# Seven block products in place of eight for the last three chunks of a gated feed-forward kernel, with the sums on VectorE

## Chip, cores, metric

One core of one Trainium2 chip. The metric is device time in microseconds (us). A profiled run also gives a span, from the first to the last recorded instruction, some 2 us shorter than the time. No die can be compared with another here.

In the lines of a profile PE is TensorE, PEld its weight loads, DVE VectorE, ACT ScalarE, POOL GpSimd and SP SyncE; `L504` is a line of the kernel. The change moves the lines: gate/value matmuls are L487 before and L505 after, gates L504 and L521, the attention multiplies that come in pairs ("the L472 pair" below) L452 and L472, the last step of `xT` L411 and L431, output products of 512 columns L514 and L530. New are the block products (L592), token sums (L586) and weight sums (L561).

## What is computed

An attention stage gives `x`, 4608 tokens of 512 features. The part that matters is the feed-forward product behind it:

```python
def _moe_ref(x, w_gate, w_val, w_out):      # 4608 x 512, 512 x 1536 (twice), 1536 x 512
    gate = np.maximum(x @ w_gate, 0.0)
    val = x @ w_val
    return (gate * val @ w_out).astype(np.float32)
```

## The kernel before

The kernel works in 36 slots. A token chunk has 512 tokens and takes four slots; each slot makes three of the chunk's twelve gate/value tiles (`emit_h`, 128 of the 1536 hidden features each) and one 128-token tile of the output product of the previous chunk (`emit_y`). Slots 0 to 27 carry attention work as well, slots 28 to 35 do not; I call these the tail. After slot 35 the last chunk's output product stands alone. A tile's gate is the step in which ScalarE and VectorE read the tile's two products out of PSUM, where the matmuls put their results in banks of 512 columns, and multiply them into SBUF. `xT` is the transposed `x` that the tiles read, in four quarters of 128 features; its last quarter is finished only 2.6 us into slot 28.

```python
def emit_h(c, jj, pp, parts=((0, range(4)), (1, range(4)))):
    h1, h2 = pair(pp)[:, 0, :], pair(pp)[:, 1, :]    # a pair is two PSUM banks
    for which, kks in parts:
        emit_h_mm(c, jj, pp, which, kks)             # 128x512 matmuls: w_gate into h1, w_val into h2
    def gate():
        r1 = ffn.tile([128, TCH], FP16, name="r1", tag="r1")
        nc.scalar.activation(out=r1, in_=h1, func=AF.Relu)
        gt = gpool.tile([128, TCH], FP16, name="gT", tag="gT")
        nc.vector.tensor_tensor(out=gt, in0=r1, in1=h2, op=ALU.mult)
        gts[c, jj] = gt
    return gate

def emit_y(c, ty, bank, cut=0, inner=None):
    # ... 12 matmuls of 512 columns into one bank, then
    nc.scalar.copy(out=y_sb, in_=y_ps)
    emit_out(c, ty, y_sb, nc.scalar)

# emit_slot, slots without attention:
    if gate: gate()                                  # third gate of the slot before
    emit_y(c - 1, s % 4, 2)
    emit_h(c, jj, 0)()                               # pair 0
    emit_h(c, jj + 1, 1)()                           # pair 1
    return emit_h(c, jj + 2, 0)                      # pair 0; its gate comes in the next slot

# after slot 35:
    gate()
    for ty in range(3):
        emit_y(NCH - 1, ty, ty)
    emit_y_last(NCH - 1, 3, 3)                       # two halves of 256 columns
```

The softmax here doesn't subtract the row's maximum and nothing guards it: scores larger than these inputs give would overflow.

## Time and profile before

| | before |
|---|---|
| time, median of 3 runs | 357.89 us (357.83 to 358.13) |
| span of the profiled run | 356.0 us |
| slot 28 starts | 279.70 us |
| last matmul starts | 352.14 us |
| TensorE busy | 97% |

### The profile page before, as it was taken

The page shows a single profiled execution, that of the slowest core. Times are in us where ns is not written, and L with a number is a line of the kernel's source. Part 1 is how long each engine was busy: PE and PEld are TensorE (multiplying, and loading weights), DVE is VectorE, ACT ScalarE, POOL GpSimd, SP SyncE. Part 2 cuts the span into 40 slices and gives each one's busy share as a digit, 9 for nine tenths or more (in the row PEclk, how much of TensorE's full clock was granted, in tenths as well). Part 3 has the DMA queues.
Part 4 walks back from the last instruction along what each step waited for, and adds up shares of the span by engine and source line. Part 5 has one row for each costly group of instructions (what it writes and reads, how often), then busy time and mean ns, then how long its engine had stood idle before and what let it go on. Part 6 is the DMA issues. An engine that isn't in the chain of part 4 may idle for free.

```text
span 356.0 us, 7222 instructions
## 1 busy us (share of the span) xinstructions
PE 346.9 (97%) x2851; PEld 177.8 (50%) x2851; DVE 226.4 (64%) x344; ACT 211.9 (60%) x358; POOL 188.7 (53%) x233
## 2 busy tenths in 40 slices
PE   6999999999999999999999999999999999999995
PEld 2665555545555455555555555555554444444443
DVE  5894666687786677777777888877775523222220
ACT  3867775676666777766666666666666532322321
POOL 8986557999999877777778877711000000000000
PEclk9999999999999999999999999999999999999999
DMA  9999999999999999999999999930000100000022
GB/s 150 168 171 187 181 196 157 176 175 180 163 166 170 154 130 130 132 130 131 129 135 133 131 133 119 119 92 31 31 30 23 38 30 29 31 29 29 31 59 89
DMA packets 167170, 40.25 MB, mean 113 GB/s; under 512 B 149888, under 2 KB 162656, under 8 KB 167136
## 3 DMA queue, kind: packets, MB, share of 16 engines
q0 software_dynamic: 132960, 22.93, 85.6%
q1 hardware_dynamic: 28832, 7.53, 15.0%
q10 hardware_dynamic: 5344, 9.34, 7.7%
q8 instruction: 22, 0.36, 0.4%
q14 instruction: 12, 0.10, 0.1%
HBM read 46.45 MB, written 9.44 MB: 157 GB/s over the span
## 4 chain that ended last, share of the span: by engine, by line
PE 90%; DVE 4%; ACT 3%; DMA 1%; issue 1%; DVEq 0%; POOLq 0%
PE ps L487 51%; PE ps L514 25%; PE ps L428 3%; PE ps L228 2%; PE ps L294 2%; PE ps L283 2%; PE ps L436 2%; DMA qk<-in_k_dram 1%; DVE xn L406 1%; ACT rden L403 1%; DVE xo L355 1%; ACT rden L405 1%; PE ps L544 1%; DVE ee L306 1%; ACT r L502 1%
## 5 line engine op out<-in xcount | busy, mean ns | idle before, releaser
L504 DVE TENSOR_TENSOR gT<-r,ps 128x512 f16<-128x512 f16 x108 | 71.9, 684 | 67.3 <-PE ps L487 45.5
L487 PE MATMUL ps<-xT,wg_sb 128*128 128x512 f16 x432 | 111.3, 379 | 0.9 <-DVE xn L406 0.8
L487 PE MATMUL ps<-xT,wv_sb 128*128 128x512 f16 x432 | 111.0, 379 | 0.0
L514 PE MATMUL ps<-wo_sb,gT 128*128 128x512 f16 x420 | 100.1, 380 | 0.0
L502 ACT ACTIVATE r<-ps 128x512 f16<-128x512 f32 x108 | 64.0, 593 | 33.5 <-PE ps L487 30.8
L452 DVE TENSOR_TENSOR xn<-ps,rden 64x720 f16<-64x720 f32 x46 | 41.6, 905 | 42.5 <-ACT rden L449 41.8
L487 PEld LDWEIGHTS <-wv_sb 128*128 128x128 f16 x432 | 42.2, 98 | 50.7
L487 PEld LDWEIGHTS <-wg_sb 128*128 128x128 f16 x432 | 39.8, 97 | 44.4 <-issue 0.7
L514 PEld LDWEIGHTS <-gT 128*128 128x128 f16 x420 | 39.1, 98 | 45.5
L303 ACT ACTIVATE ee<-ps 112x576 f16<-112x576 f32 x64 | 38.1, 647 | 26.2 <-PE ps L294 25.4
L522 ACT COPY y_sb<-ps 128x512 f32<-128x512 f32 x35 | 20.5, 587 | 46.9 <-PE ps L514 46.9
L446 ACT ACTIVATE rden<-ps 64x720 f32<-64x720 f32 x46 | 35.2, 764 | 12.8 <-PE ps L436 12.2
L306 DVE TENSOR_TENSOR ee<-ee,cst_sb 112x576 f16<-112x576 f16 x64 | 40.9, 677 | 1.3 <-ACT ee L303 1.1
L255 POOL TENSOR_TENSOR vd<-v 72x256 f16<-72x256 f32 x23 | 17.1, 745 | 44.1 <-PE ps L436 43.5
L174 POOL DMA_DIRECT2D qk<-in_q_dram x46 | 34.2, 745 | 4.3 <-DMA wo_sb<-in_moe_w_out_dram 2.8
L174 POOL DMA_DIRECT2D qk<-in_k_dram x46 | 33.3, 729 | 0.5 <-DMA vw<-in_v_dram 0.3
L195 POOL DMA_DIRECT2D vw<-in_v_dram x30 | 28.4, 948 | 4.7 <-PE ps L228 1.5
L209 DVE TENSOR_REDUCE qkd<-qkT 128x288 f16<-128x1152 f16 x23 | 30.9, 1342 | 0.0
L254 POOL TENSOR_TENSOR v<-v 72x512 f32<-72x512 f16 x23 | 30.2, 1314 | 0.3
L411 DVE TENSOR_TENSOR xT<-xn 128x576 f16<-128x576 f16 x28 | 22.4, 799 | 0.2
L428 PE MATMUL ps<-ee,vw 112*128 112x96 f16 x276 | 20.3, 205 | 0.4 <-DVE ee L306 0.4
L312 ACT ACTIVATE ed<-ps 72x576 f16<-72x576 f32 x32 | 20.5, 642 | 0.0
(77 smaller groups left out, 288.7 us busy)
## 6 DMA issues: line engine op xcount, KB each, us to landing
out_dram<-y_sb ACTq DMA_DIRECT2D x34, 256.0 KB, 3.7
vw<-in_v_dram POOLq DMA_DIRECT2D x30, 168.0 KB, 6.2
qk<-in_q_dram POOLq DMA_DIRECT2D x46, 72.0 KB, 3.6
qk<-in_k_dram POOLq DMA_DIRECT2D x46, 72.0 KB, 3.7
v<-in_v_dram POOLq DMA_DIRECT2D x23, 144.0 KB, 6.1
wg_sb<-in_moe_w_gate_dram POOLq DMA_DIRECT2D x4, 384.0 KB, 9.7
wv_sb<-in_moe_w_val_dram POOLq DMA_DIRECT2D x4, 384.0 KB, 10.5
wo_sb<-in_moe_w_out_dram POOLq DMA_DIRECT2D x4, 384.0 KB, 12.1
```

The source lines that it names most:

```text
L174: nc.gpsimd.dma_start(dv[:, :, hh, :], _dap(src, off + hh * S * D, [[D, 96], [NQ * D, NB], [1, D]]),)
L209: nc.vector.tensor_reduce(out=qkd[hp % 2].rearrange("p i t -> p (i t)"), in_=qkT[hp % 4][:, 0 : 2 * S].rearrange("p (t f) -> p t f", f=4), ...
L254: nc.gpsimd.tensor_tensor(out=m, in0=t[:, :, 0:128], in1=t[:, :, 128:256], op=ALU.add)
L303: nc.scalar.activation(out=o, in_=ps[0:WK, p0 + 2 * g : p0 + 2 * g + 2, 0:288], func=AF.Exp, scale=scale)
L306: nc.vector.tensor_tensor(out=o, in0=o, in1=_sap(masks_sb, (0, WK), 288 * g, [[0, 2], [1, 288]]), op=ALU.mult,)
L428: nc.tensor.matmul(out=ps[:, bank, NQ * j : NQ * j + NQ], lhsT=vflat[:, v0 : v0 + 128], rhs=e[:, hh, lo : lo + NQ], start=True, stop=True,)
L446: nc.scalar.activation(out=r[lo : lo + 64], in_=ps[de : de + 64, 4 + 2 * hh : 6 + 2 * hh, 0:360], func=AF.Ln)
L452: nc.vector.tensor_tensor(out=x[lo : lo + 64], in0=ps[lo : lo + 64, 4 + 2 * hh : 6 + 2 * hh, 0:360], in1=r[lo : lo + 64], op=ALU.mult,)
L487: nc.tensor.matmul(out=pair(pp)[:, which, :], lhsT=w[:, kk, bass.ts(jj, 128)], rhs=xT[:, kk, c * TCH : (c + 1) * TCH], start=(kk == 0), st ...
L502: nc.scalar.activation(out=r1, in_=h1, func=AF.Relu)
L504: nc.vector.tensor_tensor(out=gt, in0=r1, in1=h2, op=ALU.mult)
L514: nc.tensor.matmul(out=y_ps, lhsT=gts[c, jj][:, bass.ts(ty, 128)], rhs=wo_sb[:, jj, :], start=(jj == 0), stop=(jj == NJJ - 1),)
```

## The change

Intent: the output product of chunks 6, 7 and 8 as a Strassen scheme (Winograd's form). 256 tokens and 512 outputs are two by two blocks, the 1536 hidden features two halves; seven block products take the place of eight, so 42 matmuls of 256 columns do what 24 of 512 did. It needs four sums of gate blocks per 256 tokens and four sums of w_out blocks once, all fp16 on VectorE. One weight sum goes into each of slots 24 to 27, the token sums into every second slot of the tail (the last chunk's into slot 35 and behind it). Products accumulate on each other in PSUM, and ScalarE copies intermediate values out between.

```diff
-    gpool = ctx.enter_context(tc.tile_pool(name="gpool", bufs=24))
+    gT = ring(2, [128, NJJ, TCH], FP16, "gT_")           # gates of a chunk as one tile
+    wt, sa, sums = ...                                   # scratch in retired attention buffers (cut)
+    def emit_wt(i):                                      # four weight sums, 128 x 1536 each
+        o, a, b = ((t1, b12, b11), (t2, b22, t1), (t3, b22, b12), (t4, b21, t2))[i]
+        nc.vector.tensor_tensor(out=o, in0=a, in1=b, op=ALU.subtract)
+    class Unit:                                          # 256 tokens; banks a, b, d
+        def sums(self, lo=0, hi=NK, which=range(4)):     # NK = 6
+            ops = ((s1, a21, a22, ADD), (s2, s1, a11, SUB), (s3, a11, a21, SUB), (s4, a12, s2, SUB))
+            for o, a, b, op in (ops[i] for i in which):
+                nc.vector.tensor_tensor(out=o[:, lo:hi, :], in0=a[:, lo:hi, :], in1=b[:, lo:hi, :], op=op)
+        # mm(out, left, right, first): 6 matmuls of 256 columns; first clears, otherwise it accumulates
+        # p1: a = A11 B11, copied to m1          p2: d = A12 B21; y11 = d + m1
+        # p6: a += S2 T2, copied to m2           p5: b = S1 T1
+        # p7: a += S3 T3, copied to m3; y22 = b + m3
+        # p4: a += A22 T4; y21 = a               p3: b += S4 B22; y12 = b + m2
+    def emit_tail_slot(s, gate):
+        c, jj = s // 4, 3 * (s % 4)
+        gate()
+        if s % 2 == 0:
+            w = units[c - 1] = Unit(c - 1, s % 4 // 2, (4, 5, 6))
+            w.sums()
+            w.p1()
+            if s == NP - LEAD:                           # slot 28
+                emit_h_mm(c, jj, 0, 0, range(3))
+                emit_h_mm(c, jj, 0, 1, range(3))
+                w.p2()
+                emit_h(c, jj, 0, ((0, range(3, 4)), (1, range(3, 4))))()
+            else:
+                emit_h(c, jj, 0)(); w.p2()
+            emit_h(c, jj + 1, 1)()
+            w.p6(); w.p5()
+        else:
+            # ... p7, tile jj, p4, tile jj + 1, p3; in slot 35 also last[0].sums(0, 4), last[1].sums(0, 4)
+        return emit_h(c, jj + 2, 0)
     # after slot 35
-    for ty in range(3):
-        emit_y(NCH - 1, ty, ty)
-    emit_y_last(NCH - 1, 3, 3)
+    # p1 of both units, the sums' slices 4 and 5, then p2, p6, p5, p7, p4, p3, each for both units
```

More of the change, by code (lines that the diff above doesn't have):

```diff
@@ L85 @@
     NVP = 9
+    NK = NJJ // 2
     B0 = 1
@@ L94 @@
     ffn = ctx.enter_context(tc.tile_pool(name="ffn", bufs=3))
-    gpool = ctx.enter_context(tc.tile_pool(name="gpool", bufs=24))
+    ypool = ctx.enter_context(tc.tile_pool(name="ypool", bufs=4))
     zero_sb = keep.tile([128, 640], FP16, name="zero_sb")
@@ L112 @@
     NV4 = 5
-    qk16 = ring(NL, [96, 2, 2 * NB * 64], FP16, "qk16_")
+    qkfull = ring(NL, [128, 2, 2 * NB * 64], FP16, "qk16_")
+    qk16 = [t[0:96] for t in qkfull]
     v4 = ring(NV4, [72, 4, 256], FP16, "v4_")
-    v2 = ring(2, [72, 4, 128], FP32, "v2_")
-    vw = ring(NL, [WK, 2 * NB, 128], FP16, "vw_")
+    v2full = ring(2, [128, 4, 128], FP32, "v2_")
+    v2 = [t[0:72] for t in v2full]
+    vwfull = ring(NL, [128, 2 * NB, 128], FP16, "vw_")
+    vw = [t[0:WK] for t in vwfull]
     qkT = ring(4, [128, 2 * S + 32], FP16, "qkT_")
@@ L125 @@
     ones_sb = keep.tile([128, 128], FP16, name="ones_sb")
-    q32 = keep.tile([96, 2 * NB * 64], FP32, name="q32")
+    q32full = keep.tile([128, 2 * NB * 64], FP32, name="q32")
+    q32 = q32full[0:96]
+    gT = ring(2, [128, NJJ, TCH], FP16, "gT_")
     xT = keep.tile([128, NPB, NTOK], FP16, name="xT")
     ps = psum.tile([128, 8, 512], FP32, name="ps")
+    wt = [
+        t.rearrange("p i c -> p (i c)").rearrange("p (j d) -> p j d", d=256) for t in qkfull[0:4]
+    ]
+    sa = [
+        [vwfull[r].rearrange("p b c -> p (b c)")[:, 768 * i : 768 * (i + 1)]
+         .rearrange("p (j t) -> p j t", t=128) for r in rs for i in range(2)]
+        for rs in ((4, 5), (6, 0))
+    ]
+    v2flat = [t.rearrange("p a b -> p (a b)") for t in v2full]
+    sums = [
+        [q32full[:, 256 * i : 256 * (i + 1)] for i in range(3)],
+        [v2flat[0][:, 0:256], v2flat[0][:, 256:512], v2flat[1][:, 0:256]],
+    ]
     nc.scalar.preload_act_table_set("natural_log_exp_and_others")
@@ L480, in emit_x_pe @@
             nc.vector.tensor_copy(out=o, in_=pair(pp)[:, :, 0:288])
-    gts = {}
     def emit_h_mm(c, jj, pp, which, kks):
@@ L502, in gate @@
             nc.scalar.activation(out=r1, in_=h1, func=AF.Relu)
-            gt = gpool.tile([128, TCH], FP16, name="gT", tag="gT")
-            nc.vector.tensor_tensor(out=gt, in0=r1, in1=h2, op=ALU.mult)
-            gts[c, jj] = gt
+            nc.vector.tensor_tensor(out=gT[c % 2][:, jj, :], in0=r1, in1=h2, op=ALU.mult)
         return gate
@@ L515, in emit_y @@
                 out=y_ps,
-                lhsT=gts[c, jj][:, bass.ts(ty, 128)],
+                lhsT=gT[c % 2][:, jj, bass.ts(ty, 128)],
                 rhs=wo_sb[:, jj, :],
@@ L520, in emit_y @@
             )
-        y_sb = ffn.tile([128, D_MODEL], FP32, name="y_sb", tag="y_sb")
+        y_sb = ypool.tile([128, D_MODEL], FP32, name="y_sb", tag="y_sb")
         nc.scalar.copy(out=y_sb, in_=y_ps)
@@ L535, in emit_out @@
             done += n
-    def emit_y_last(c, ty, bank):
-        y_sb = ffn.tile([128, D_MODEL], FP32, name="y_sb", tag="y_sb")
-        for i, (copy, eng) in enumerate(
-            ((nc.scalar.copy, nc.scalar), (nc.vector.tensor_copy, nc.sync))
-        ):
-            lo, hi = 256 * i, 256 * i + 256
-            for jj in range(NJJ):
-                nc.tensor.matmul(
-                    out=ps[:, bank + i, 0:256],
-                    lhsT=gts[c, jj][:, bass.ts(ty, 128)],
-                    rhs=wo_sb[:, jj, lo:hi],
-                    start=(jj == 0),
-                    stop=(jj == NJJ - 1),
-                )
-            copy(out=y_sb[:, lo:hi], in_=ps[:, bank + i, 0:256])
-            emit_out(c, ty, y_sb, eng, lo, hi)
+    halves = [
+        [wo_sb[:, NK * i : NK * (i + 1), 256 * k : 256 * (k + 1)] for k in range(2)] for i in range(2)
+    ]
@@ new lines, in emit_wt, with __init__, mm, p1 @@
+    def emit_wt(i):
+        (b11, b12), (b21, b22) = halves
+        t1, t2, t3, t4 = wt
+        o, a, b = ((t1, b12, b11), (t2, b22, t1), (t3, b22, b12), (t4, b21, t2))[i]
+        nc.vector.tensor_tensor(out=o, in0=a, in1=b, op=ALU.subtract)
+    class Unit:
+        def __init__(self, c, u, banks):
+            self.c, self.u = c, u
+            self.a, self.b, self.d = (ps[:, k, 0:256] for k in banks)
+            self.s1, self.s2, self.s3, self.s4 = sa[u]
+            self.m1, self.m2, self.m3 = sums[u]
+            g = gT[c % 2]
+            self.x = [
+                [g[:, NK * i : NK * (i + 1), 256 * u + 128 * t : 256 * u + 128 * t + 128] for i in range(2)]
+                for t in range(2)
+            ]
+        def sums(self, lo=0, hi=NK, which=range(4)):
+            (a11, a12), (a21, a22) = self.x
+            ops = (
+                (self.s1, a21, a22, ALU.add),
+                (self.s2, self.s1, a11, ALU.subtract),
+                (self.s3, a11, a21, ALU.subtract),
+                (self.s4, a12, self.s2, ALU.subtract),
+            )
+            for o, a, b, op in (ops[i] for i in which):
+                nc.vector.tensor_tensor(
+                    out=o[:, lo:hi, :], in0=a[:, lo:hi, :], in1=b[:, lo:hi, :], op=op
+                )
+        def mm(self, out, left, right, first):
+            for i in range(NK):
+                nc.tensor.matmul(
+                    out=out,
+                    lhsT=left[:, i, :],
+                    rhs=right[:, i, :],
+                    start=(first and i == 0),
+                    stop=(i == NK - 1),
+                    skip_group_check=True,
+                )
+        def p1(self):
+            self.y = [
+                ypool.tile([128, D_MODEL], FP32, name="y_sb", tag="y_sb") for _ in range(2)
+            ]
+            self.mm(self.a, self.x[0][0], halves[0][0], True)
+            nc.scalar.copy(out=self.m1, in_=self.a)
+        def p2(self):
+            self.mm(self.d, self.x[0][1], halves[1][0], True)
+            nc.vector.tensor_tensor(out=self.y[0][:, 0:256], in0=self.d, in1=self.m1, op=ALU.add)
+            self.out(0, 0)
+        def p6(self):
+            self.mm(self.a, self.s2, wt[1], False)
+            nc.scalar.copy(out=self.m2, in_=self.a)
+        def p5(self):
+            self.mm(self.b, self.s1, wt[0], True)
+        def p7(self):
+            self.mm(self.a, self.s3, wt[2], False)
+            nc.scalar.copy(out=self.m3, in_=self.a)
+            nc.vector.tensor_tensor(out=self.y[1][:, 256:512], in0=self.b, in1=self.m3, op=ALU.add)
+            self.out(1, 1)
+        def p4(self):
+            self.mm(self.a, self.x[1][1], wt[3], False)
+            nc.scalar.copy(out=self.y[1][:, 0:256], in_=self.a)
+            self.out(1, 0)
+        def p3(self):
+            self.mm(self.b, self.s4, halves[1][1], False)
+            nc.vector.tensor_tensor(out=self.y[0][:, 256:512], in0=self.b, in1=self.m2, op=ALU.add)
+            self.out(0, 1)
+        def out(self, t, k):
+            emit_out(self.c, 2 * self.u + t, self.y[t], nc.sync, 256 * k, 256 * k + 256)
@@ L599, in emit_fill @@
         emit_warm(1)
+    units = {}
+    def emit_tail_slot(s, gate):
[11 more added lines that the diff above has]
+            else:
+                emit_h(c, jj, 0)()
+                w.p2()
+            emit_h(c, jj + 1, 1)()
+            w.p6()
+            w.p5()
+        else:
+            w = units[c - 1]
+            w.p7()
+            emit_h(c, jj, 0)()
+            w.p4()
+            if s == 4 * NCH - 1:
+                last[0].sums(0, 4)
+            emit_h(c, jj + 1, 1)()
+            w.p3()
+            if s == 4 * NCH - 1:
+                last[1].sums(0, 4)
+        return emit_h(c, jj + 2, 0)
     def emit_slot(s, gate):
@@ L636, in emit_slot @@
             emit_h(c, jj, 0)()
+            if 24 <= s < 28:
+                emit_wt(s - 24)
             if hp < NP:
@@ L673 @@
         gate = None
-        for s in range(NCH * 4):
+        for s in range(NP - LEAD):
             gate = emit_slot(s, gate)
+        gate = lambda: None
+        last = [Unit(NCH - 1, u, b) for u, b in ((0, (4, 5, 6)), (1, (7, 2, 3)))]
+        for s in range(NP - LEAD, NCH * 4):
+            gate = emit_tail_slot(s, gate)
         gate()
-        for ty in range(3):
-            emit_y(NCH - 1, ty, ty)
-        emit_y_last(NCH - 1, 3, 3)
+        for x in last:
+            x.p1()
+        for which in (range(2), range(2, 4)):
+            for x in last:
+                x.sums(4, NK, which)
+        for p in ("p2", "p6", "p5", "p7", "p4", "p3"):
+            for x in last:
+                getattr(x, p)()
 _INS = ['q', 'k', 'v', 'moe_w_gate', 'moe_w_val', 'moe_w_out']
```

## The prediction

> **What bounds the kernel now.** I began with the page, parts 1, 2 and 4: busy time, the slices, and the chain of work that ended last.
>
> ```profile
> PE 346.9 (97%) x2851; PEld 177.8 (50%) x2851; DVE 226.4 (64%) x344; ACT 211.9 (60%) x358; POOL 188.7 (53%) x233
> ...
> DVE  5894666687786677777777888877775523222220
> ...
> PEclk9999999999999999999999999999999999999999
> ...
> PE 90%; DVE 4%; ACT 3%; DMA 1%; issue 1%; DVEq 0%; POOLq 0%
> PE ps L487 51%; PE ps L514 25%; PE ps L428 3%; PE ps L228 2%; PE ps L294 2%; PE ps L283 2%; PE ps L436 2%; DMA qk<-in_k_dram 1%; DVE xn L406 1%; ACT rden L403 1%; DVE xo L355 1%; ACT rden L405 1%; PE ps L544 1%; DVE ee L306 1%; ACT r L502 1%
> ```
>
> The reader is to see that TensorE is busy 97% of the span at full clock and that 90% of the last chain is TensorE work. A matmul taken away shortens the kernel, so long as nothing else fills its place. VectorE falls to two or three tenths in the last eight to nine slices, which are the stage that the change fills. That stage begins at 279.70 us (slot 28 of 36, the first without attention) and reads like this in the timeline of the last 26 us:
>
> ```profile
> 339.27 1.03 PE L487 MATMUL ps<-xT,wv_sb 128*128 128x512 f16 x4
> ...
> 341.86 7.93 PE L514 MATMUL ps<-wo_sb,gT 128*128 128x512 f16 x36
> 342.13 0.69 DVE L504 TENSOR_TENSOR gT<-r,ps 128x512 f16<-128x512 f16 x1 [1.04 <-PE ps L487]
> ...
> 349.42 2.72 PEld L544 LDWEIGHTS <-gT 128*128 128x128 f16 x24
> 349.63 2.78 PE L544 MATMUL ps<-wo_sb,gT 128*128 128x256 f16 x24
> ...
> 352.50 0.42 DVE L551 COPY y_sb<-ps 128x256 f32<-128x256 f32 x1 [9.69 <-DMA out_dram<-y_sb]
> 352.96 0.34 SPq L531 DMA_DIRECT2D out_dram<-y_sb  x1
> ```
>
> From this come the two prices that matter. The length shown for a group includes the latency of its last matmul (means 379 ns at 512 columns, 272 ns at 256, in the groups by line). So one 512-column matmul takes (7.93 - 0.38)/35 = 0.2157 us from start to start, and one of 256 columns (2.78 - 0.27)/23 = 0.1091 us: half, with no penalty. Weight loads are 98 ns each, under 109, so they still hide, narrowly. The output of the last product ends at 352.25; copy, DMA and the closing barrier bring the span to 356.0, a tail of 3.75 us.
>
> For VectorE the page's mean misleads, and I asked for the groups by form between 240 and 280 us:
>
> ```profile
> L504 DVE TENSOR_TENSOR gT<-r,ps 128x512 f16<-128x512 f16 x12 | 7.9, 685 | 3.9 <-PE ps L487 3.0 <-ACT r L502 0.7
> L306 DVE TENSOR_TENSOR ee<-ee,cst_sb 112x576 f16<-112x576 f16 x8 | 3.3, 452 | 0.0
> L411 DVE TENSOR_TENSOR xT<-xn 128x576 f16<-128x576 f16 x4 | 3.0, 752 | 0.0
> ```
>
> An fp16 sum of 576 elements out of SBUF takes 452 ns here (677 on the page, whose mean includes the GpSimd-heavy part), where the same length with a broadcast operand takes 752.
>
> **What the Trainium skill says.** "TensorE: Matmul & The Clock Gate", section "Wait — 56ns, not 53.3ns?": warm start-to-start is N/2.4 GHz plus about 2.5 ns. That gives 215.8 and 109.2 ns; the trace agrees. "VectorE: DVE Perf Modes", section "What auto-detection actually checks": a tensor_tensor whose tensors are all 16-bit with unit step runs at two elements per cycle. The trace agrees: 452 against 752 ns. Every weight sum and token sum of the change has this form (fp16, unit innermost step). "SBUF — State Buffer", section "Who interferes with whom": VectorE operations with two SBUF inputs and GpSimd operations that read SBUF exclude each other. The inflated 677 ns mean fits this; GpSimd shows no work after 258 us, so the token sums should not be held.
>
> **The change, part by part.**
>
> *Removed and put in, TensorE.* One unit is 256 tokens by 512 outputs. Before: 2 x 12 matmuls of 512 columns, 24 x 0.2157 = 5.18 us. After: 7 products x 6 matmuls of 256 columns, 42 x 0.1091 = 4.58 us. Six units (chunks 6, 7, 8): 6 x 0.60 = 3.6 us. The scheme saves 1/8 of these matmuls' time and adds no weight-load time. The combinations of products accumulate in PSUM by starting without a clear, at no matmul cost.
>
> *Added, VectorE, hidden.* From the 452 ns I take (N/2 + 145)/0.96. Four weight sums of 1536 elements cost 0.95 us each, one in each of slots 24 to 27. The instruction order puts each between a gate multiply and the L452 pair, where VectorE idles about 2 us waiting for ScalarE's reciprocal (10.2 us over ten instructions, all before the first of each pair). So 0.95 us fits, and even 1.75 us at one element per cycle would.
>
> Four token sums per unit, 768 elements: 0.55 us each, about 2.1 us together, in every second slot of the tail. That slot lasts 3 x 1.73 + 4 x 0.65 = 7.8 us and VectorE has 3 gates (2.1 us), one 256-column output sum (0.42) and the sums (2.1): 4.6 of 7.8. The gate that frees the next PSUM pair is ordered ahead of the sums. The next gate is late by about 0.6 us, but its second bank is wanted only 3 us later. The first product P1 reads raw gates and P6 is two gate/value pairs later, so neither waits for the sums.
>
> *Slot 28.* Here xT's last quarter comes late, at 282.30 us before. The new order covers it with P1, six matmuls of the first three quarters and P2: 0.65 + 1.29 + 0.65 = 2.6 us from 279.70, just to 282.3. I allow 0 to 0.1 us of wait.
>
> *Last slot and end.* VectorE must do gate 9, four sums of 512 elements (about 1.5 us), gate 10, an output sum, four more sums and gate 11. Taking slot 35's start as zero: gate 9 is ready at 2.65 and done at 3.34, sums to 4.85, gate 10 from 5.03 to 5.72, output sum to 6.15, sums to 7.65, gate 11 to 8.3. TensorE ends its value matmuls at 7.13, runs P1 of both units to 8.44, and asks for gate 11 only in the sixth matmul of P2, at 9.0. A margin of 0.7 us. The remaining slices of the sums are eight of 256 elements (0.28 us each), of which P6 wants only the first four, at 9.75 or later. Afterwards the two units alternate, so a PSUM bank has 0.65 us to be read by ScalarE (0.20 to start, 0.37 for the copy) before it is accumulated on again: 0.57 plus a semaphore, about even. Allow 0.1 us for both units.
>
> The last chunk's matmuls are 84 x 0.1091 = 9.16 us, against 36 x 0.2157 + 24 x 0.1091 = 10.38: this 1.2 is already in the 3.6. Then comes an output sum of 256 columns from PSUM (0.42 us, as the 512-column multiply's 685 ns scales), where a copy of 0.42 us was, and the same 128 KB DMA from SP. So the tail stays 3.75 us, give or take 0.2. Output DMAs come every 0.65 us at the end, with SP issues of 0.34 us; they keep up.
>
> Sum: -3.6 TensorE, +0.1 slot 28, +0.1 the interleaved end, about 0 tail: -3.4 to -3.5 us. 357.9 - 3.5 = **354.4 us**, 1% less. Scratch tiles reuse attention buffers after their last use, so nothing earlier should move.
>
> **Rivals.** *(a) VectorE becomes the bound in the tail.* If fp16 sums ran at one element per cycle, 768 elements would be 0.95 us and the even slot's VectorE 6.3 us, still under 7.8. But in slot 35, gate 11 would end near 9.4 instead of 8.3 and TensorE would stall about 0.5 us: 355.0. L306's 452 ns speaks against it; the strided halves of w_out and gates have the same unit inner step, but no instruction of before has just these patterns.
>
> *(b) The narrow matmuls do not hold 109 ns.* If weight loads (98 ns) stopped hiding behind 109 ns, for instance with semaphore waits standing on loads, each narrow matmul would cost 10 to 20 ns more. Then 252 x 10 to 20 ns = 2.5 to 5 us, and the gain would be gone: 356.9 to 359.4. The 24 matmuls of L544 speak against it, as they ran two groups back to back without a gap.
>
> *(c) The end is longer.* Eight small outputs, each waiting for an in-order SP queue, and the chain PSUM, ScalarE copy, VectorE add before most of them. If the end's DMA work lagged by one or two issues it would cost 0.3 to 0.8 us: 354.7 to 355.2. Before, 256 KB landed 3.7 us after issue and 128 KB 1.7 to 2.3, against a need of 128 KB each 0.65 us; the mean at the end was below 100 GB/s where the first half moved up to 196, so bandwidth is there.
>
> **Range and chances.** The saving is bounded: 3.6 us is all that the matmuls give, 1.0% of the time, so more than 2% faster (under 350.7) would need something unseen. Slower by over 2% would need 7 us of new waits in 76 us of tail. Most of the doubt is on the side of small waits, hence a lopsided range: 353.8 to 355.6. Faster 0.02, within 2% 0.96, slower 0.02.
>
> **What would show it.** In the profile after: 252 matmuls of 128x256 with group lengths that give 109 ns from start to start; pairs of tail slots of about 14.9 us, where they were 15.5; TensorE idle time after 280 us below 0.4 us in all; token sums near 550 ns and weight sums near 950; last matmul about 3.5 us earlier and 3.75 us from it to the end. Wrong it would be if TensorE shows waits for VectorE gates or sums in the last slot, if 256-column matmuls start more than 115 ns apart, if slots 24 to 27 lengthen, or if the time from the last matmul to the end grows.

## More of the kernel before

One more view is needed for comparison later: the busy time by stretch, from slot 28's start to the last matmul's start. Its columns are the stretch, its length, then the busy us (and instructions) of TensorE, TensorE's weight loads, VectorE, ScalarE and GpSimd, then the granted clock, the DMA share and GB/s.

```profile
279.70:352.14 72.44, 72.44 (x348) 33.97 (x347) 19.07 (x28) 21.14 (x36) 0.00 (x0) 1.00 0.11 41
```

TensorE has no idle time in these 72.44 us, while VectorE works for only 19.

## The result

| | before | after |
|---|---|---|
| time, median | 357.88 us (4 runs, 357.83 to 358.13) | 354.56 us (4 runs, 354.10 to 355.57) |
| span of the profiled run | 356.0 | 352.6 |
| start to slot 28 | 279.70 | 279.39 |
| slot 28 to the last matmul's start | 72.44 | 69.54 |
| last matmul's start to the end | 3.85 | 3.65 |

The ratio is 0.9903, interval 0.9876 to 0.9929. A ratio is the mean time of one kernel's fast runs over that of the other's of the same rounds, so it is not quite the ratio of the medians. The predicted 354.4 us is 0.2 us off.

The page of the changed kernel, parts 1, 2 and 4, to be held against the lines in the prediction:

```profile
PE 343.5 (97%) x2947; PEld 187.0 (53%) x2947; DVE 248.3 (70%) x397; ACT 214.0 (61%) x370; POOL 189.5 (54%) x233
...
DVE  5894666687786677788887787776777655354581
...
PE 89%; DVE 4%; ACT 4%; DMA 1%; issue 1%; POOLq 0%
```

TensorE is 3.4 us less busy, with 96 more and narrower matmuls. VectorE has gained 22 us of work, and its share in the tail is up from two or three tenths to three to eight. It still is not the bound: TensorE's share of the chain is 89%.

The tail by stretch, same columns as before, and TensorE's waits in it (who waited for whom, us in total, times, longest):

```profile
279.39:348.93 69.54, 69.02 (x445) 43.32 (x443) 37.61 (x77) 23.26 (x48) 0.00 (x0) 1.00 0.12 39
```

```profile
PE ps L505 <- DVE gT L521: 0.5, 1, 0.5
```

Every other matmul in the tail starts on time, but for one that is 0.02 us late at 346.9. This one did not. The same place before the change, lines of slots 27 and 28:

```profile
278.47 1.84 DVE L452 TENSOR_TENSOR xn<-ps,rden 64x720 f16<-64x720 f32 x2 [2.05 <-ACT rden L449]
...
279.70 2.75 PE L514 MATMUL ps<-wo_sb,gT 128*128 128x512 f16 x12
280.35 1.28 DVE L504 TENSOR_TENSOR gT<-r,ps 128x512 f16<-128x512 f16 x2
281.55 0.75 DVE L411 TENSOR_TENSOR xT<-xn 128x576 f16<-128x576 f16 x1
...
283.15 1.03 PE L487 MATMUL ps<-xT,wv_sb 128*128 128x512 f16 x4
```

And of the changed kernel:

```profile
278.16 1.84 DVE L472 TENSOR_TENSOR xn<-ps,rden 64x720 f16<-64x720 f32 x2 [1.19 <-ACT rden L469]
...
279.39 0.82 PE L592 MATMUL ps<-wo_sb,gT 128*128 128x256 f16 x6
280.03 1.28 DVE L521 TENSOR_TENSOR gT<-r,ps 128x512 f16<-128x512 f16 x2
280.04 0.81 PE L505 MATMUL ps<-xT,wg_sb 128*128 128x512 f16 x3
...
281.23 0.75 DVE L431 TENSOR_TENSOR xT<-xn 128x576 f16<-128x576 f16 x1
281.37 0.81 PE L505 MATMUL ps<-xT,wv_sb 128*128 128x512 f16 x3 [0.52 <-DVE gT L521]
281.90 0.55 DVE L586 TENSOR_TENSOR vw<-gT 128x768 f16<-128x768 f16 x1
282.02 0.82 PE L592 MATMUL ps<-wo_sb,gT 128*128 128x256 f16 x6
282.49 0.56 DVE L586 TENSOR_TENSOR vw<-vw,gT 128x768 f16<-128x768 f16 x1
282.67 0.38 PE L505 MATMUL ps<-xT,wg_sb 128*128 128x512 f16 x1
282.89 0.38 PE L505 MATMUL ps<-xT,wv_sb 128*128 128x512 f16 x1
282.96 0.55 DVE L586 TENSOR_TENSOR vw<-gT 128x768 f16<-128x768 f16 x1
```

After P1 (279.39) come three w_gate matmuls at 280.04, 216 ns each from start to start, so the first w_val matmul could begin at 280.69. It begins at 281.37, 0.68 us later. (The view says 0.52, because it counts the last matmul's latency as busy.) It writes the second bank of pair 0. The two gates at 280.03 are gates 10 and 11 of slot 27, and gate 11 reads just that bank until 281.31. Before the change, 2.6 us of output product stood between: gate 11 ended at 281.63, the bank was written from 283.15, and nothing waited.

The last chunk's products and their VectorE neighbours ran without a wait:

```profile
339.85 2.78 PE L592 MATMUL ps<-wo_sb,gT 128*128 128x256 f16 x24
340.13 0.68 DVE L521 TENSOR_TENSOR gT<-r,ps 128x512 f16<-128x512 f16 x1
...
347.73 1.47 PE L592 MATMUL ps<-wo_sb,vw 128*128 128x256 f16 x12
```

### The profile page after: what moved, and what is told of

Same layout as the page of the kernel before. It is cut to its first block, busy times and chain, and to the rows that moved or that the text cites. A ratio compares the mean times of both kernels' runs of the same rounds, so it can differ in the third digit from the quotient of the medians.

```text
span 352.6 us, 7540 instructions
## 1 busy us (share of the span) xinstructions
PE 343.5 (97%) x2947; PEld 187.0 (53%) x2947; DVE 248.3 (70%) x397; ACT 214.0 (61%) x370; POOL 189.5 (54%) x233
## 4 chain that ended last, share of the span: by engine, by line
PE 89%; DVE 4%; ACT 4%; DMA 1%; issue 1%; POOLq 0%
PE ps L505 50%; PE ps L530 18%; PE ps L592 8%; PE ps L448 3%; PE ps L248 2%; PE ps L314 2%; PE ps L303 2%; PE ps L456 2%; DMA qk<-in_k_dram 1%; DVE xn L426 1%; ACT rden L423 1%; DVE xo L375 1%; ACT rden L425 1%; DVE ee L326 1%; ACT r L520 1%
## 5 line engine op out<-in xcount | busy, mean ns | idle before, releaser
L530 PE MATMUL ps<-wo_sb,gT 128*128 128x512 f16 x288 | 70.1, 380 | 0.0
L472 DVE TENSOR_TENSOR xn<-ps,rden 64x720 f16<-64x720 f32 x46 | 41.6, 905 | 39.2 <-ACT rden L469 38.5
L530 PEld LDWEIGHTS <-gT 128*128 128x128 f16 x288 | 26.1, 98 | 30.0
L538 ACT COPY y_sb<-ps 128x512 f32<-128x512 f32 x24 | 14.1, 587 | 17.2 <-PE ps L530 17.2
```

Of the source, the lines that this page charges most:

```text
L472: nc.vector.tensor_tensor(out=x[lo : lo + 64], in0=ps[lo : lo + 64, 4 + 2 * hh : 6 + 2 * hh, 0:360], in1=r[lo : lo + 64], op=ALU.mult,)
L530: nc.tensor.matmul(out=y_ps, lhsT=gT[c % 2][:, jj, bass.ts(ty, 128)], rhs=wo_sb[:, jj, :], start=(jj == 0), stop=(jj == NJJ - 1),)
```

## The experiments

The time of one run moves by a microsecond or more, and the runs came in three batches on different chips (the first four below, the next four, the last two). The changed kernel ran beside the first and the last batch; in the second only the kernel before did, at 357.76 us. I therefore read each experiment mainly from its trace, from slot 28's start to the last matmul's start, called the tail stretch below. In the four profiles that have the changed tail untouched (the changed kernel three times, and the one with the moved weight sum) it was 69.54 us each time.

**The changed kernel again.**

> The changed kernel again, as the yardstick for the runs beside it and for its spread. Its first four runs lay between 354.1 and 355.6 us where the kernel before lay within 0.3 us. Theory: the spread is in the first microseconds, where the first loads land; the tail from slot 28 on is the same in every profile (73.2 us). Rival: the spread is a wait in the new tail. If the tail is 73.2 us again within 0.1, the first holds.

354.68 us median of 6 runs (353.96 to 356.84), ratio 0.9923. The tail stretch is 69.54 and the rest to the end 3.65 us, as before. Slot 28 started at 279.64 us, against 279.39. Over all twelve profiles it started between 278.88 and 280.78 us, and the 26th matmul, among the first that wait for loaded k, between 6.48 and 7.37 us. In the three profiles of the changed kernel slot 28 follows that matmul by 272.81 to 272.83 us, so their spread is all in the first microseconds, and the first holds for them. In the other builds the distance is 272.40 to 273.94 us: ahead of the tail too, but not only the first loads. The unprofiled runs have no trace.

**Another pair order in slot 28.**

```diff
-                emit_h_mm(c, jj, 0, 0, range(3))
-                emit_h_mm(c, jj, 0, 1, range(3))
+                emit_h_mm(c, jj, 1, 0, range(3))
+                emit_h_mm(c, jj, 1, 1, range(3))
                 # and pair 1 for the rest of this tile, 0 for the next, 1 for the third, in slot 28 only
```

> Slot 28 uses the PSUM pairs in the order 1, 0, 1 instead of 0, 1, 0. Theory: the one TensorE wait of the new tail (0.68 us at 280.5 us) is for the bank of pair 0 that gate 11 of slot 27 still reads; pair 1 was read by gate 10, which ends 0.6 us earlier, so the wait goes and the time falls by 0.6 to 0.7 us to about 353.8. Rival: what is late in slot 28 is VectorE's whole chain (gate 11, then xT's last quarter), so the wait moves to P2 or to the fourth quarter and the time changes by less than 0.2 us.

The tail stretch is 68.94 us, 0.60 less, and TensorE is busy for all of it in this view:

```profile
280.31:349.25 68.94, 68.94 (x444) 43.34 (x443) 37.54 (x77) 23.26 (x48) 0.00 (x0) 1.00 0.12 39
```

Its timeline shows why: the w_val matmuls now follow the w_gate ones directly, beside gate 11.

```profile
280.96 1.29 DVE L521 TENSOR_TENSOR gT<-r,ps 128x512 f16<-128x512 f16 x2
280.97 0.81 PE L505 MATMUL ps<-xT,wg_sb 128*128 128x512 f16 x3
...
281.70 0.81 PE L505 MATMUL ps<-xT,wv_sb 128*128 128x512 f16 x3
```

They begin 0.73 us after the w_gate ones, where three matmuls take 0.65, so under 0.1 us of the wait is left. The rival, that xT or P2 would wait instead, is out. The time is another matter: 354.52 us (353.80 to 356.99), against 354.68 beside it. The predicted 353.8 was not seen as a median. In the profiled run (354.67) slot 28 began at 280.31 us, 0.67 later than beside it, which takes up the gain; why the unprofiled runs are no faster is not shown.

**The fourth weight sum one slot earlier.**

```diff
-            if 24 <= s < 28:
+            if 24 <= s < 27:
                 emit_wt(s - 24)
+            if s == 26:
+                emit_wt(3)
```

> The fourth weight sum moves from slot 27 to slot 26, which then has two. Theory: the weight sum lies in VectorE's wait for ScalarE's reciprocal and delays nothing; the 0.68 us wait in slot 28 stays and the time is that of the changed kernel within 0.1 us. Slot 26 gets 1.9 us of sums into a gap of 2.06 us, so it should not lengthen. Rival: the weight sum pushes slot 27's gates back and so causes the wait; then the wait shrinks by up to 0.68 us and the time with it.

355.10 us (354.51 to 356.27), 0.42 above the changed kernel beside it where 0.1 was expected; the ranges overlap, and I read the trace. The tail stretch is 69.54 and the wait is there unchanged. With no weight sum in slot 27, VectorE's idle time ahead of the L472 pair is 2.05 us, where it was 1.19: the sum lay in idle time that ScalarE's reciprocal imposed. The rival is out, and this weight sum is shown to be free. For all four the two main profiles say it: slots 24 to 27 take 36.65 us together before and after.

```profile
278.55 1.84 DVE L472 TENSOR_TENSOR xn<-ps,rden 64x720 f16<-64x720 f32 x2 [2.05 <-ACT rden L469]
...
281.76 0.81 PE L505 MATMUL ps<-xT,wv_sb 128*128 128x512 f16 x3 [0.52 <-DVE gT L521]
```

**P1 twice in slot 28.**

```diff
+            if s == NP - LEAD:
+                w.mm(w.a, w.x[0][0], halves[0][0], True)
             w.p1()
```

> In slot 28 alone, product P1 runs twice (the second clears and repeats it, so the result is right): six more matmuls, 0.65 us of TensorE work ahead of the waiting matmul. Theory: they fill the 0.68 us wait, and the time is that of the changed kernel within 0.1 us. Rival: if the wait is set by work that follows TensorE, it moves with it and the time grows by 0.65 us.

354.89 us (354.14 to 355.22), 0.21 above the changed kernel, again more than the 0.1 expected and within the spread. Six more matmuls, and the tail stretch is the same 69.54 us, now all busy: the wait took them in whole.

```profile
280.26:349.80 69.54, 69.54 (x450) 43.91 (x449) 37.63 (x77) 23.26 (x48) 0.00 (x0) 1.00 0.12 39
```

With the pair order, this settles what the wait is for: a time set by VectorE, and a bank, not something behind TensorE's own work.

**Token sums twice, except in the last slot.**

```diff
-            for o, a, b, op in (ops[i] for i in which):
+            for o, a, b, op in (ops[i] for i in which for _ in range(2 if hi - lo == NK else 1)):
```

> In slots 28, 30, 32 and 34 every token sum runs twice in a row (same result): about 2.1 us more VectorE work in each of these slots, 8.4 us in all. The last slot's sums stay single. Theory: VectorE has over 3 us of room in these slots, so from slot 28's start to the last matmul stays at 69.54 us, with at most 0.3 us more in slot 28, where the sums begin late. Rival: VectorE is near the bound in the tail; then each slot grows by 1 us or more and the time by 4 us or more.

354.98 us (354.17 to 356.17).

```profile
278.88:348.76 69.88, 69.18 (x445) 43.34 (x443) 46.22 (x93) 23.28 (x48) 0.00 (x0) 1.00 0.12 39
```

VectorE works 8.6 us more (46.22 against 37.61) and the tail stretch grows by 0.34, a little over the 0.3 allowed. All of it is one new wait in slot 28, where the sums begin late:

```profile
286.84 1.02 PE L505 MATMUL ps<-xT,wv_sb 128*128 128x512 f16 x4 [0.17 <-DVE gT L521]
```

The matmul should start at 286.50 (the view counts the latency of the one ahead as busy, as above). Slots 30, 32 and 34 take the doubled sums at no cost. VectorE is not near the bound there.

**The last slot's sums twice.**

```diff
-            for o, a, b, op in (ops[i] for i in which):
+            for o, a, b, op in (ops[i] for i in which for _ in range(2 if lo == 0 and hi == 4 else 1)):
```

> In the last slot alone the eight sums of 512 elements run twice: 3 us more VectorE work ahead of gate 11. Theory: here the room is small, 0.85 us between gate 11's end and the matmul of P2 that reads it; TensorE then waits 2.0 to 2.4 us and the time grows by so much. Rival: the sums are as well hidden here as in the other slots: under 0.3 us.

357.21 us (356.87 to 359.52): the whole gain over the kernel before is gone, ratio 0.9996.

```profile
279.76:351.98 72.22, 69.20 (x445) 43.24 (x443) 40.98 (x85) 23.28 (x48) 0.00 (x0) 1.00 0.11 38
```

```profile
PE ps L592 <- DVE gT L521: 2.5, 1, 2.5
PE ps L505 <- DVE gT L521: 0.5, 1, 0.5
```

The end of gate 11 and the matmul that it held up:

```profile
344.00 0.68 DVE L521 TENSOR_TENSOR gT<-r,ps 128x512 f16<-128x512 f16 x1
...
344.74 0.50 PE L592 MATMUL ps<-wo_sb,gT 128*128 128x256 f16 x3 [2.49 <-DVE gT L521]
```

The tail stretch grows by 2.67 us, a little over the 2.0 to 2.4 that I wrote. Counted from slot 28's start, gate 11 ends at 64.92 us, where it ended at 61.43: 3.49 us later, not the 3 that I had put in. TensorE waited 2.66 us for it, so the room that gate 11 has ahead of P2 is 0.83 us. The 0.85 of the expectation was right, the added work was not.

**P2 twice in every unit.**

```diff
-            self.mm(self.d, self.x[0][1], halves[1][0], True)
+            for _ in range(2):
+                self.mm(self.d, self.x[0][1], halves[1][0], True)
```

> Product P2 runs twice in all six units (the second clears and repeats it): the eighth product of the plain scheme in time, with everything else kept: 36 more matmuls of 256 columns. Theory: the gain is the removed matmuls alone, each on the path that sets the end: 36 x 0.109 = 3.9 us more from slot 28's start to the last matmul (73.5 us). Rival: part of the gain is something else (shorter groups, outputs in halves, other queues); then clearly less than 3.9.

359.63 us (358.70 to 361.05), ratio 1.0062. The tail stretch is 73.48 us, 3.94 more: 36 matmuls at 0.109.

```profile
279.86:353.34 73.48, 72.95 (x481) 46.86 (x479) 38.14 (x77) 23.28 (x48) 0.00 (x0) 1.00 0.11 37
```

The eighth product costs its matmuls in full, so removing it gains them in full. Beside the kernel before, its tail stretch is 1.04 us longer: it has as many columns to stream, in narrower matmuls, and the 0.68 us wait in slot 28 too.

**The last chunk as before.**

```diff
-        # p1 ... p3 of both units, and their sums in slot 35
+        for ty in range(3):
+            emit_y(NCH - 1, ty, ty)
+        emit_y_last(NCH - 1, 3, 3)
```

> Chunks 6 and 7 keep the seven products; the last chunk's product and its outputs are as in the kernel before. Theory: its share of the gain, 10.38 - 9.16 = 1.2 us, is lost from slot 28's start to the last matmul (70.8 us), and the time from the last matmul to the end goes back from 3.65 to 3.85 us, because outputs come from two queues again and more closing waits are left for after the last landing. Rival: if the dependent sums and copies at the end eat the gain there, under 0.5 us is lost.

356.02 us (355.41 to 357.02), ratio 0.9952. The tail stretch is 70.74 us, 1.20 more, just the difference of the matmuls.

```profile
280.78:351.52 70.74, 70.22 (x420) 41.01 (x419) 31.05 (x56) 22.43 (x44) 0.00 (x0) 1.00 0.12 42
```

So the copies and dependent sums at the end ate nothing. From the last matmul to the end it was 3.72 us, not the 3.85 of the kernel before, so the outputs' queues explain about a third of the 0.20 us there.

**The pair order and the changed kernel once more.**

> The pair order 1, 0, 1 in slot 28 once more, beside the changed kernel on one chip, because the first timing of both (354.52 and 354.68 us) could not tell 0.6 us apart. Theory: the trace again has 68.94 us from slot 28's start to the last matmul, and the median is 0.3 to 0.9 us under the changed kernel's; runs differ by 1 us or more because of the first loads, so the intervals may still overlap. Rival: what the tail gains is lost elsewhere in the unprofiled runs, and the medians agree.

> The changed kernel, as the yardstick of the run beside it: 69.54 us from slot 28's start to the last matmul, and a median between 354.3 and 355.0 us.

The pair order: 354.72 us (354.01 to 355.65), ratio 0.9902, tail stretch 68.95. The changed kernel: 355.07 us (354.44 to 355.45), ratio 0.9913, tail stretch 69.54. The medians differ by 0.35 us in the expected direction, yet the intervals overlap. Over all runs, the batches put together, the means are 354.88 (11 runs, standard error 0.30) and 354.96 (15 runs, 0.19): not told apart. What is shown is 0.6 us in the tail of both profiles. It did not reach the time of either profiled run (354.67 against 354.62, 354.72 against 354.44), because slot 28 began 0.67 and 0.91 us later than in the changed kernel beside it. Both profiles were among the three with the latest 26th matmul (7.14 and 7.37 us), and slot 28 followed that matmul 0.2 to 0.4 us later than in the changed kernel. So the rival, that the gain is lost elsewhere, is not out: whether that is chance, or the build shifts the first loads, stays open.

## Why the prediction was right

The time and the range held, but one term was mis-sized, and two terms that I had set to about zero hid it.

| term | predicted | measured in the two profiles |
|---|---|---|
| matmuls taken away | -3.6 | -3.60 (tail -2.90, with waits of 0.68 and 0.02 us taken out) |
| slot 28 | 0 to +0.1 | +0.68 |
| interleaved end | +0.1 | +0.02 |
| last matmul's start to the end | 0, give or take 0.2 | -0.20 |
| start to slot 28 | 0 | -0.31 |
| sum | -3.4 to -3.5 | -3.41 |

- *The price of a narrow matmul.* Right: 109 ns from start to start also with the new operands, and each on the path. P2 twice shows it with 36 matmuls (+3.94), the plain last chunk with a third of the gain (+1.20, as worked out). The weight loads did grow, from 33.97 to 43.32 us in the tail, where I wrote that none are added, but they stayed hidden. Rival (b) is out.
- *VectorE's sums hidden.* Right. Token sums took 552 ns for 0.55 predicted, weight sums 950 ns for 0.95, so the two-elements-per-cycle reading of L306 carried over to strided blocks, as the Trainium skill ("VectorE: DVE Perf Modes", section "What auto-detection actually checks") has it. Doubling them in slots 28 to 34 cost 0.34 us of 8.6. The formula (N/2 + 145)/0.96 behind them comes out of two lines, 452 and 752 ns, not of the 452 alone: at one and at two elements per step, 576 elements differ by 288 steps and by 300 ns. Rival (a) is out at this speed. My sum for it was too low: by the same formula eight sums of 512 elements would each take 0.27 us longer at one element per step, some 2.1 us in all, which puts gate 11 near 10.2 and the stall near 1.2 us (an estimate), not at 9.4 and 0.5.
- *Gate 11's margin in the last slot.* Predicted 0.7 us; doubling the sums there showed 0.83, so it was right and a little on the safe side.
- *Slot 28.* This is the step that failed. I checked the cover for xT's late last quarter and took it for the only late input; the wait that I put at 0 to 0.1 us measured 0.68. The gates of slot 27 are late for the same reason, behind the L472 pair, and the tile started under that cover writes the bank that gate 11 still reads. My sentence that the gate which frees the next pair is ordered ahead of the sums is true and did not help: gate 11 stands behind gate 10 and the L472 pair, and only P1 and three matmuls stand ahead of its bank on TensorE. The rule that TensorE must not write a bank that VectorE reads, by bank, is in the Trainium skill ("PSUM — Partial Sum Buffer", section "PSUM bank collisions raise a hardware error"); the trace shows the kernel keeping it, at 0.68 us.
- *The signs that I had named.* None of those that would have shown me wrong came. Two of the others missed: TensorE's waits after 280 us are 0.70 us in all, where I wrote under 0.4, and the last matmul came 3.21 us earlier, not about 3.5. Both are slot 28's wait.
- *Start and end.* Of the 0.31 us at the start, 0.19 is where the first loads happened to land (the 26th matmul at 6.77 and 6.58 us), and 0.12 is one attention matmul near 74 us (it waited 0.4 us before and 0.3 after); the twelve profiles differ by 1.9 us in slot 28's start. Of the 0.20 us at the end I can say only that it was there in every profile of the changed product (3.64 or 3.65) and mostly (3.72) with the last chunk as before. What makes it is not settled.

Without these two the span would have come out at about 353.1 (352.6 + 0.31 + 0.20), 0.5 us above what I worked out. So the hit on the time to 0.2 us was partly luck, two terms against a third; the mechanism and its main term were not.

## What to carry to other kernels

When a block of matmuls is shortened, ask what else it used to cover: every bank that the next matmuls write, and not only the input that is known to be late. An eighth of the multiplications can be bought with sums on an idle engine if each sum lies well ahead of its reader, and the place to check is the one where the gates feed the product at once: here the last slot had 0.83 us of room, while slots 30, 32 and 34 took twice the sums for nothing. A gain of a few tenths that lies behind a noisy start is read from a stretch of the trace that starts after the noise, here repeatable to about 0.01 us.

## What the Trainium skill lacked or had wrong

- "VectorE: DVE Perf Modes", section "The DRAIN you can't avoid", says of eight copies on VectorE that a semaphore after each costs nothing extra. That does not carry over to these sums. Here two fp16 sums of 768 elements started 0.59 us apart where the second waits for the first (281.90 and 282.49), and 0.47 us apart where it does not (282.49 and 282.96): the wait costs 0.12 us, and where there is none an operation starts before the one ahead has ended (0.56 us long). The second half agrees with the same section's remark that a next operation which is not held starts earlier.
- No page that I read gives the spread of the first loads from run to run. Here the 26th matmul started between 6.48 and 7.37 us, and the time of one and the same kernel moved between 353.96 and 356.84 us; how much of that is the first loads is not shown.
